# Two spectrum products in one instruction, with a new order of side jobs and ring slots, in an S4 and bilinear GLU block

## The chip, the cores and the metric

The kernel runs on one core of one Trainium2 chip. The metric is device time in microseconds for one execution. The kernel before takes 987.09 us, the median of three runs (984.9, 987.09 and 990.64).

## The reference

All inputs are fp32; there is one sequence of L = 2048 tokens with D = 640 channels, N = 192 complex states per channel and a hidden width F = 1536. Cut to what matters:

```python
mod = silu(c) @ w_mod                        # 640 -> 6 x 640: sa, ca, ga, sb, cb, gb
h = layernorm(x) * (1 + ca) + sa
# S4: for each channel d a kernel of 2048 taps, then a long convolution
P = exp(dt[d] * A[d, n] * l)                 # l = 0 .. 2047, complex
K[d, l] = Re(sum_n C[d, n] * P[d, n, l] * dt * B[d, n])
y = irfft(rfft(pad(h)) * rfft(pad(K)))[:2048] + h * Dskip
x = x + ga * y
h = layernorm(x) * (1 + cb) + sb
x = x + gb * (((h @ w_gate) * (h @ w_up)) @ w_down)
```

## The kernel before

The channels are worked in 5 blocks of 128 (db = 0 to 4). The program has four stretches.

**Start.** Constants, dt, seeds of the exponentials for channel block 0, loads of slices of w_mod, loads of rows of x. For a modulation vector, `mod_l` (L354) loads one third-dimension slice of w_mod, 1600 KB, into the memory that later holds a table (`t_tw` or `t_ti`), and `modrow` (L361) multiplies it on TensorE in two pieces, half 0 with 384 columns and half 1 with 256; ScalarE then copies each piece out.

**Kernel generation.** It has 40 steps, each for 16 channels; a step is three turns of the loop `for t in range(3*NK+24)` near L1335. In a step GpSimd forms outer products: the phases `Ph` as int32 and the magnitudes `EQ` and `EP` as fp32 (`outer`, L714), for the next step. ScalarE takes sines of the phases (`trig`, all ScalarE work is recorded at L230) into `tr`. VectorE multiplies sines by magnitudes into `QtA`, `PtA`, `QtB`, `PtB` (L769 to L796); L769 reads one operand twice through a broadcast. TensorE contracts over the states (L811 and L826). `Ph`, `EQ` and `EP` have two buffers each, so GpSimd waits where ScalarE or VectorE has not read them out. At the beginning of each channel block the seeds are made (`u_seeds`, 14 pieces on VectorE, ScalarE and TensorE, the last with three loads of ScalarE's activation table), and GpSimd doubles small tables from them (`tab_ph`, `tab_eq`).

**Side jobs.** All else of the convolution runs between these, as generators: each `yield` ends a piece. `u_stats` and `u_hm` load a block of 128 rows of x (320 KB), take its statistics on VectorE (L477) and store the normalised rows. `u_pre` (L853) is the first stage of the forward transform of the input, `u_g` (L899) its second, `u_k` (L838) the first stage of a kernel's transform. `u_c` (L919) does the second stage of the kernel's transform on TensorE (`stage2`, L893, which reads the table `t_tw`), the complex product with the input's spectrum on VectorE (L934 to L940), the first inverse stage on TensorE (L950), a copy on ScalarE and a store to `WD` in DRAM (L955). There are 16 whole ones and, for block 4, four that go in two halves. `u_d` (L958) reloads from `WD` (L963), does the last inverse stage (L971) and adds the residual (L978, or L975 into `xb`). `tables` (L1250) loads `t_tw`, once the last modulation slice there has been used.

The order is written out by hand in numbers. `SCHED` has a due time for each piece of each job; 60 units are a step, 20 a turn, and negative ones lie in the start. At each turn the pieces whose time has come are issued, in order of their numbers:

```python
(kg_aq, kg_ap, kg_b)[g](n)      # ScalarE: sines
due(2 * t)                      # side jobs
for f in MUL.pop(0): f()        # VectorE: products
due(2 * t + 1)                  # side jobs
kg_pool(n + 1, g)               # GpSimd: outer products, then TensorE
```

Each engine, and each engine's DMA queue, works in the order of issue. `SLOT` gives, letter by letter, which buffer of a ring the next tile of that name gets (`psf` in PSUM, `TV`, `gh`, `hf`, `W`, `xs`, `Kt` in SBUF); a tile waits until the last user of its buffer is done.

**Tail and GLU.** After the 40 steps 24 more turns (due times 2400 to 2880) do the rest of the convolution. Beside it the first weights are loaded by SP (`raw`, L1004, 640 KB), split into a high and a low part on ScalarE and VectorE (`split_g`, L1026), and the statistics of the first tokens taken (L1139). `split_g` of weight 1 also issues the next raw load. Then the GLU follows with its own hand-written order: products in L1078, L1502 and L1554 on TensorE.

In the product of a spectrum block, `kr` and `ki` are two PSUM tiles of 128 x 4 x dn (dn is 128, or 64 in block 4), `H` the input's spectrum and `T` a tile of the ring `TV`:

```python
V.tensor_tensor(T[:, 0], kr, H[:, 0], op=OP.mult)   # L934
V.tensor_tensor(T[:, 1], kr, H[:, 1], op=OP.mult)   # L935
V.tensor_tensor(kr, ki, H[:, 1], op=OP.mult)        # L936
V.tensor_tensor(ki, ki, H[:, 0], op=OP.mult)        # L937
V.tensor_tensor(x[:, 0], T[:, 0], kr, op=OP.subtract)
V.tensor_tensor(x[:, 1], T[:, 1], ki, op=OP.add)
```

## Time and profile before

| | us |
|---|---|
| median of the three runs | 987.09 |
| the profiled execution: its time | 988.54 |
| the profiled execution: its span | 986.8 |
| TensorE (PE) busy | 889.2 (90%) |
| VectorE (DVE) busy | 723.8 (73%) |
| ScalarE (ACT) busy | 579.4 (59%) |
| GpSimd (POOL) busy | 509.1 (52%) |

The span runs from the first to the last instruction on record; the time is the device's. The granted TensorE clock was 0.961 of full speed on the mean. The page cuts the span in 40 slices of 24.7 us and gives each engine's busy share as a digit in tenths. PEld is TensorE's weight load, which overlaps PE. In a row of a timeline stand the start, the duration, the engine, the line, the operation, the output and inputs with their shape, a count, and in brackets the idle time of the engine before it and what ended it. A name such as SPq or ACTq is a DMA issued by that engine.

### The profile page before, as it was taken

What the parts mean: (1) busy time and instruction counts of PE and PEld (TensorE: products, weight loads), DVE (VectorE), ACT (ScalarE), POOL (GpSimd) and SP (SyncE); (2) the same over time, 40 slices, a digit from 0 to 9 for tenths busy, and PEclk for the clock granted to TensorE, in tenths of its full rate; (3) what the DMA queues carried; (4) which work ended last, traced back from release to release, by engine and by line L of the source; (5) the groups of instructions that cost most, each with busy time, mean ns of one, the idle gap of its engine ahead of it and who ended that gap; (6) DMA issues with size and microseconds to landing.
All of it is one profiled execution on the core that took longest, in us unless ns stands there. A gap on an engine that the chain in (4) does not pass through costs nothing.

```text
span 986.8 us, 26765 instructions
## 1 busy us (share of the span) xinstructions
PE 889.2 (90%) x11134; PEld 720.2 (73%) x11134; DVE 723.8 (73%) x1400; ACT 579.4 (59%) x1076; POOL 509.1 (52%) x400
## 2 busy tenths in 40 slices
PE   4867898799789789988879999999999999999998
PEld 3565556586476557667736888889999788888998
DVE  8789568888978888794857665457676756578952
ACT  4869989987888887863336333334355443435430
POOL 5978899699879979960030354440113122222110
PEclk9877979999989889999999999999999999999999
DMA  7746654556246534658595665733564676658875
GB/s 254 262 142 223 204 194 147 172 165 185 77 153 181 152 105 126 205 172 257 189 273 191 222 191 182 242 125 113 184 217 124 197 231 222 222 179 292 237 244 187
DMA packets 158817, 188.54 MB, mean 191 GB/s; under 512 B 9828, under 2 KB 128360, under 8 KB 157544
## 3 DMA queue, kind: packets, MB, share of 16 engines
q1 hardware_dynamic: 149480, 155.51, 49.4%
q0 software_dynamic: 4752, 21.63, 7.6%
q10 hardware_dynamic: 4464, 9.70, 2.6%
q8 instruction: 87, 1.43, 0.6%
q14 instruction: 34, 0.28, 0.1%
HBM read 124.22 MB, written 62.59 MB: 189 GB/s over the span
## 4 chain that ended last, share of the span: by engine, by line
PE 55%; DVE 14%; ACT 12%; issue 10%; POOL 4%; DMA 3%; SPq 0%; DVEq 0%; POOLq 0%; ACTq 0%
PE pa L1078 18%; PE psg L1078 9%; PE pa L1502 9%; PE psfc L893 2%; PE kg L826 2%; PE kg L811 2%; PE psfa L893 2%; PE psfb L893 2%; ACT trb L230 1%; ACT tra L230 1%; PE psfc L950 1%; POOL EQ L714 1%; PE psfb L950 1%; PE pa L1554 1%; ACT L230 1%
## 5 line engine op out<-in xcount | busy, mean ns | idle before, releaser
L1055 POOL TENSOR_TENSOR tf<-wur,wgb 128x256 f32<-128x256 f32 x23 | 17.8, 775 | 246.9 <-DVE wtl L1026 199.5
L714 POOL TENSOR_TENSOR EQ<-LQ,RH 128x1536 f32<-128x1536 f32 x40 | 124.1, 3104 | 9.7 <-DVE QtB L771 9.5
L1026 DVE TENSOR_TENSOR wtl<-tf,wth 128x256 fp32r<-128x256 f32 (+1 forms) x72 | 36.7, 513 | 59.7 <-ACT wth L230 59.7
L714 POOL TENSOR_TENSOR Phb<-LH,DH 128x1536 int32<-128x1536 int32 x20 | 62.2, 3112 | 13.9 <-ACT tra L230 13.9
L714 POOL TENSOR_TENSOR EP<-LP,RH 128x768 f32<-128x768 f32 x40 | 66.0, 1650 | 0.0
L714 POOL TENSOR_TENSOR Pha<-LH,DH 128x1536 int32<-128x1536 int32 (+1 forms) x21 | 62.4, 2971 | 2.3 <-ACT trb L230 2.0
L1502 PE MATMUL pa<-wsg,sh 128*128 128x384 f32 (+1 forms) x304 | 58.4, 311 | 0.0
L826 PE MATMUL kg<-QtB,PtB 64*32 64x64 f32 x2560 | 48.7, 229 | 5.8 <-DVE QtB L770 5.3
L826 PEld LDWEIGHTS kg<-QtB,PtB 64*32 64x32 f32 x2560 | 41.7, 114 | 16.1 <-issue 7.2
L1502 PEld LDWEIGHTS pa<-wsg,sh 128*128 128x128 f32 x304 | 45.7, 189 | 0.0
L1541 POOL DMA_DIRECT2D wsg<-wdc x21 | 11.2, 531 | 66.5 <-PE pa L1554 35.6
L1026 DVE TENSOR_TENSOR wsg<-wga,wsg 128x640 fp32r<-128x640 f32 x36 | 33.7, 943 | 13.8 <-ACT wsg L230 13.8
L230 ACT ACTIVATE sh<-a 128x512 fp32r<-128x512 f32 x55 | 33.3, 625 | 13.9 <-PE psg L1554 6.2
L230 ACT ACTIVATE wsg<-wga 128x640 fp32r<-128x640 f32 x36 | 26.1, 730 | 25.0 <-PE pa L1502 12.8
L1026 DVE TENSOR_TENSOR sl<-a,sh 128x512 fp32r<-128x512 f32 x55 | 37.5, 702 | 4.0 <-ACT sh L230 4.0
L1078 PE MATMUL pa<-hh,wsg 128*128 128x512 f32 x150 | 40.2, 394 | 0.0
L1148 POOL TENSOR_SCALAR hfa<-xb,hr,hr 128x128 f32<-128x128 f32 x4 | 2.3, 577 | 67.5 <-DVE hr L283 67.5
L230 ACT ACTIVATE s<-pa 128x512 f32<-128x512 f32 x12 | 7.2, 598 | 48.5 <-PE pa L1078 48.5
L769 DVE TENSOR_TENSOR QtA<-tra,EQ 128x1024 f32<-128x1024 f32 x20 | 24.4, 1220 | 15.0 <-PE kg L811 7.0
L230 ACT ACTIVATE wth<-tf 128x256 fp32r<-128x256 f32 (+1 forms) x72 | 32.5, 481 | 4.9 <-DVE tf L1056 1.8
L230 ACT ACTIVATE a<-pa 128x512 f32<-128x512 f32 x12 | 7.2, 598 | 47.7 <-PE pa L1078 47.7
L1502 PE MATMUL pa<-wsg,sl 128*128 128x384 f32 (+1 forms) x152 | 34.4, 308 | 0.0
(656 smaller groups left out, 3125.6 us busy)
## 6 DMA issues: line engine op xcount, KB each, us to landing
wsg<-wdc POOLq DMA_DIRECT2D x21, 640.0 KB, 5.3
wgb<-B_w_gate SPq DMA_DIRECT2D x24, 320.0 KB, 4.6
wur<-B_w_up SPq DMA_DIRECT2D x24, 320.0 KB, 5.8
wsd<-wsg SPq DMA_DIRECT2D x12, 640.0 KB, 3.9
wga<-wdg SPq DMA_DIRECT2D x12, 640.0 KB, 3.9
wsg<-wsd POOLq DMA_DIRECT2D x12, 640.0 KB, 4.9
wdc<-xb SPq DMA_DIRECT2D x21, 320.0 KB, 3.3
TVb<-WD SPq DMA_DIRECT2D x22, 256.0 KB, 3.5
```

The lines of the kernel that those rows point to most:

```text
L230: return S.activation(o, i, f, **kw)
L714: G.tensor_tensor(o.rearrange("p x (h l) -> p x h l", l=8), lo.unsqueeze(2).to_broadcast([P, rows, nh, 8]), hi.rearrange("p h x -> p x h") ...
L769: return [lambda: V.tensor_tensor(Qt[:, :, :, 0:32], tr[:, :, :, ::-1], e[:, :, 0:32].unsqueeze(1).to_broadcast([P, 2, R, 32]), op=OP.mult ...
L811: PE.matmul(kg[j * 32 : j * 32 + 32, dd, :], PtA[:, c, dl * 4 + j, :], QtA[:, c, dl * 4 + j, :], start=dd == 0 and c == 0, stop=False, til ...
L826: PE.matmul(kg[j * 32 : j * 32 + 32, dd, :], PtB[lo : lo + 64, c, r, :], QtB[lo : lo + 64, c, r, :], start=False, stop=dd == 7 and c == 1, ...
L893: PE.matmul(r[c][par * 64 : par * 64 + 64, i, :], t_tw[:, k0 + k, c, :], src[:, k, :], start=True, stop=True, tile_position=(0, par * 64))
L950: PE.matmul(r[par][:, i], t_ti[lo : lo + 64, qd * 4 + i, c, :], x[lo : lo + 64, c, i, :], start=c == 0, stop=c == 1, tile_position=(lo, 0))
L1026: V.tensor_tensor(lo, v, hi, op=OP.subtract)
L1055: E.tensor_tensor(t[:, 0:2], u[:, 0:2], g[:, 0:2], op=OP.subtract)
L1078: PE.matmul(ps, w[a][:, k], x[b][:, l], start=first and n == 0 and m == 0, stop=n == 2 and m == len(ks) - 1, skip_group_check=True)
L1502: PE.matmul(AC[tb][t][c], x[:, ts], w[:, cs], start=st, stop=f == NF - 1 and n == 2 and (c == 0 or t % 2 == 1))
L1541: G.dma_start(WD[q], wdc[:, q // 3, q % 3])
```

## The change

In `u_c` the two products with `kr` become one instruction of double length, with `kr` read twice through a broadcast: 16 times 128 x 1024 in place of two of 128 x 512, and 8 times 128 x 512 in place of two of 128 x 256. In `SCHED` nearly every due time is new, and in `SLOT` most letters. The jobs themselves, their pieces and the order of pieces within a job stay as they were, and so does the GLU. What moves: in the start, half 0 of a modulation row (`mr`, third pair) comes before half 1, and the loads of two slices of w_mod (`ml`) come ahead of all blocks of x (`st`) but one; `t_tw` (`tab`) is loaded at 666 and not at 487, with the first `u_g` using it at 720 (before 710); of the three `u_c` products in steps 28 to 31 (block 2) one goes from 1688 to 1678 and one from 1919 to 1929, and the last seed pieces of block 4 (`q`, fourth row) from 1773, 1775 and 1800 to 1761, 1767 and 1818; kernel transform 37 goes ahead of step 40; in the tail the reloads of block 4 (`d`, last row) come at 2740 and 2765, before the second piece of weight work (`w`, fourth number, 2806).

```diff
@@ -29,148 +29,153 @@
 TURN = float(np.float32(2.0 * math.pi / 2.0**32 * (1.0 - 1.5e-7)))
 
 SCHED = dict(
-    ml=(-885, -929, -989),
-    mr=(((98, 154), (90, 130)), ((-884, 78), (-877, 73)), ((-885, -881), (-889, 132))),
+    ml=(-883, -955, -988),
+    mr=(((122, 153), (76, 101)), ((-878, 59), (-875, 116)), ((-888, -862), (-888, 22))),
     st=(
-        (-955, 11),
-        (-929, 195),
-        (-874, 149),
-        (-925, 128),
-        (-938, 121),
-        (-879, 152),
-        (-869, 167),
-        (-924, 162),
-        (-995, -925),
-        (-938, -871),
-        (-885, 93),
-        (-990, -871),
-        (50, 180),
-        (51, 214),
-        (-930, -878),
-        (-927, 39),
+        (-903, 20),
+        (-952, 164),
+        (-922, 78),
+        (-883, 75),
+        (-937, 55),
+        (-875, 104),
+        (-877, 153),
+        (-865, 126),
+        (-1003, -887),
+        (-944, -872),
+        (-934, 41),
+        (-950, -872),
+        (73, 158),
+        (153, 182),
+        (-947, -873),
+        (-911, 32),
     ),
...
-    rstd=(228, 229),
-    tab=(487, 829),
-    fo=(157, 189, 197, 222),
-    e0=(138,),
-    ds=(250, 255, 397, 411),
-    mc=((-872, 289, 307, 356, 356), (217, 378, 439, 446, 461), (309, 570, 620)),
+    rstd=(194, 195),
+    tab=(666, 794),
+    fo=(166, 179, 181, 182),
+    e0=(143,),
+    ds=(339, 319, 492, 204),
+    mc=((-866, 181, 279, 300, 324), (295, 337, 454, 508, 555), (343, 543, 593)),
     q=(
-        (-869, 185, 203, 222, 239, 309, 337, 355, 356, 357, 357, 358, 368, 369),
-        (338, 577, 594, 672, 676, 688, 718, 745, 812, 816, 825, 855, 872, 872),
-        (989, 1089, 1237, 1248, 1250, 1264, 1295, 1295, 1327, 1332, 1349, 1349, 1350, 1366),
-        (1298, 1403, 1490, 1732, 1735, 1735, 1746, 1763, 1773, 1775, 1778, 1800, 1830, 1835),
+        (-863, 160, 179, 224, 268, 273, 311, 316, 349, 349, 352, 352, 362, 369),
+        (448, 516, 635, 710, 717, 717, 722, 748, 800, 819, 822, 822, 833, 864),
+        (980, 1121, 1236, 1259, 1265, 1265, 1287, 1304, 1333, 1336, 1341, 1345, 1345, 1348),
+        (1286, 1415, 1599, 1728, 1737, 1737, 1746, 1751, 1761, 1767, 1786, 1818, 1828, 1837),
     ),
...
     c=(
-        ((814, 827, 901, 920), (780, 811, 971, 994), (1037, 1061, 1087, 1119), (912, 937, 1081, 1096)),
-        ((1383, 1400, 1462, 1484), (1183, 1207, 1352, 1373), (1331, 1337, 1371, 1385), (1104, 1141, 1221, 1239)),
-        ((1871, 1899, 2040, 2059), (1582, 1599, 1636, 1660), (1667, 1688, 1807, 1838), (1911, 1919, 2064, 2075)),
-        ((2088, 2090, 2133, 2146), (2187, 2210, 2277, 2289), (2348, 2351, 2395, 2412), (2295, 2310, 2343, 2346)),
-        ((2424, 2671, 2681, 2693, 2697, 2801), (2410, 2550, 2551, 2632, 2671, 2758), (2442, 2496, 2691, 2701, 2758, 2801), (2399, 2519, 2543, 2613, 2613, 2722)),
+        ((808, 828, 946, 946), (790, 815, 972, 994), (1053, 1064, 1091, 1108), (949, 963, 1081, 1087)),
+        ((1428, 1435, 1480, 1491), (1182, 1206, 1381, 1400), (1318, 1334, 1412, 1428), (1131, 1142, 1205, 1234)),
+        ((1863, 1885, 1973, 1991), (1603, 1603, 1622, 1668), (1643, 1678, 1816, 1830), (1915, 1929, 1997, 2036)),
+        ((2075, 2081, 2105, 2110), (2193, 2210, 2252, 2284), (2347, 2367, 2398, 2425), (2291, 2316, 2340, 2354)),
+        (
+            (2430, 2644, 2657, 2683, 2691, 2713),
+            (2401, 2563, 2601, 2602, 2642, 2666),
+            (2482, 2551, 2677, 2686, 2700, 2721),
+            (2373, 2457, 2610, 2636, 2664, 2667),
+        ),
     ),
     d=(
-        ((1839, 1887, 1907), (1356, 1450, 1450), (2879, 2879, 2879), (1143, 1182, 1199)),
-        ((1485, 1572, 1572), (1546, 1590, 1611), (1713, 1840, 1858), (1678, 1747, 1774)),
-        ((2151, 2257, 2269), (2245, 2320, 2328), (2323, 2396, 2422), (2119, 2149, 2168)),
-        ((2450, 2483, 2549), (2497, 2543, 2606), (2753, 2798, 2852), (2574, 2665, 2678)),
-        ((2816, 2835, 2861), (2847, 2876, 2876), (2862, 2877, 2878), (2876, 2879, 2879)),
+        ((1635, 1677, 1727), (1368, 1473, 1499), (2818, 2837, 2856), (1137, 1171, 1173)),
+        ((1760, 1801, 1806), (1548, 1610, 1645), (1827, 1897, 1958), (1712, 1729, 1763)),
+        ((2105, 2181, 2181), (2044, 2088, 2104), (2235, 2252, 2267), (2092, 2123, 2147)),
+        ((2523, 2558, 2589), (2586, 2612, 2634), (2720, 2767, 2813), (2609, 2709, 2724)),
+        ((2740, 2805, 2816), (2765, 2824, 2828), (2857, 2873, 2877), (2836, 2869, 2875)),
     ),
     k=(
...
-        (2504, 2534),
-        (2413, 2437),
-        (2492, 2495),
-        (2495, 2507),
...
+        (2446, 2513),
+        (2347, 2417),
+        (2519, 2586),
+        (2509, 2549),
     ),
...
-    w=(2508, 2575, 2790, 2776, 2819, 2829),
-    wl=(2444, 2450),
-    wm=(2801, 2834),
-    h=(2480, 2716, 2875, 2876, 2878, 2878, 2878, 2878),
...
+    w=(2456, 2588, 2714, 2806, 2783, 2709),
+    wl=(2554, 2672),
+    wm=(2795, 2810),
+    h=(2658, 2781, 2825, 2833, 2833, 2847, 2859, 2866),
...
-    Kt="abababaababbbabaabab",
...
-    W="abbababababababababababab",
...
+    W="ababababababababababababa",
...
-    xs="ababababababababbbab",
...
+    Kt="abababababbaabababab",
...
+    xs="ababababababababbaba",
 )
 SEG0 = ("l", "a", "b", "c", "ud", "r", "x", "e", "f", "G", "g", "D", "h", "v", "R", "")
 SEG = ("l", "a", "b", "c", "ud", "D", "r", "R", "x", "eE", "f", "g", "h", "v")
@@ -931,8 +936,7 @@
             need(1, "GH", db, qd)
             H = GH[db, qd][..., d0 : d0 + dn]
             T = ring(fp, [P, 2, 4, dn], "TV")
-            V.tensor_tensor(T[:, 0], kr, H[:, 0], op=OP.mult)
-            V.tensor_tensor(T[:, 1], kr, H[:, 1], op=OP.mult)
+            V.tensor_tensor(T, kr.unsqueeze(1).to_broadcast([P, 2, 4, dn]), H, op=OP.mult)
             V.tensor_tensor(kr, ki, H[:, 1], op=OP.mult)
             V.tensor_tensor(ki, ki, H[:, 0], op=OP.mult)
             x = T if parts == 1 else H
```

More of the change, by code (lines that the diff above doesn't have):

```diff
@@ new lines @@
+    hm=(
+        (46, 289),
+        (250, 415),
+        (276, 306),
+        (-1010, 384),
+        (-1007, 214),
+        (109, 286),
+        (92, 233),
+        (-871, 241),
+        (302, 355),
+        (228, 297),
+        (265, 316),
+        (201, 219),
+        (355, 512),
+        (241, 452),
+        (491, 539),
+        (373, 467),
+    ),
+    rstd=(194, 195),
[4 more added lines that the diff above has]
+    mc=((-866, 181, 279, 300, 324), (295, 337, 454, 508, 555), (343, 543, 593)),
```

106 lines of the change are left out of this document (45 added, 61 removed), and 20 rows, old and new, of tables (g, pre).

## The prediction

> **What bounds the kernel now.** I read the page's head and slices, then busy time by stage, then each engine's timeline and the chain of waits. The page:
>
> ```profile
> span 986.8 us, 26765 instructions
> ...
> POOL 5978899699879979960030354440113122222110
> ```
>
> GpSimd (POOL) is near full for 17 of 40 slices, about 24.7 us each, and light after that. The stages, with PE, PEld, DVE, ACT and POOL busy, then clock, DMA share and GB/s:
>
> ```profile
> 0.00:24.00 24.00, 9.87 (x37) 7.14 (x38) 19.52 (x86) 12.00 (x24) 12.19 (x26) 1.00 0.79 250
> 24.00:436.00 412.00, 348.66 (x7636) 256.91 (x7636) 346.60 (x619) 344.47 (x630) 371.99 (x222) 0.91 0.53 167
> 436.00:527.00 91.00, 75.38 (x1072) 54.55 (x1070) 58.42 (x154) 35.21 (x63) 9.36 (x15) 0.98 0.77 236
> 527.00:987.00 460.00, 455.33 (x2396) 401.55 (x2394) 299.22 (x544) 187.68 (x360) 115.58 (x138) 1.00 0.62 200
> ```
>
> The last 460 us, the GLU, are TensorE work (455 busy). The change touches none of it, so it counts at zero and moves only with its start. Three stages are left: the start, the 40 kernel-generation steps (24 to 436), and the tail between them and the GLU. In the generation GpSimd is busy 372 of 412 us (90%), the other three about 84% each. No GpSimd instruction is added or removed, so only its 40 idle us can be won there. The largest idle times (in brackets, with the releaser):
>
> ```profile
> 75.38 3.11 POOL L714 TENSOR_TENSOR EQ<-LQ,RH 128x1536 f32<-128x1536 f32 x1 [6.04 <-DVE QtB L771]
> 181.39 3.11 POOL L714 TENSOR_TENSOR Phb<-LH,DH 128x1536 int32<-128x1536 int32 x1 [5.95 <-ACT tra L230]
> 277.61 0.38 POOL L654 TENSOR_TENSOR DL<-ptb 128x96 int32<-128x96 int32 x1 [7.26 <-issue]
> 351.93 3.12 POOL L714 TENSOR_TENSOR Phb<-LH,DH 128x1536 int32<-128x1536 int32 x1 [6.35 <-ACT tra L230]
> ```
>
> Four waits make 25.6 of the 40 us. The last of them follows a block of seed work on ScalarE:
>
> ```profile
> 341.01 1.28 ACT L230 ACT_TABLE_LOAD   x1
> ...
> 349.89 1.28 ACT L230 ACT_TABLE_LOAD   x1
> 351.19 0.60 ACT L230 ACTIVATE tra<-Phb 128x512 f32<-128x512 int32 x1
> ```
>
> From 341.0 to 351.2 ScalarE makes seeds of the next channel block; the sines on which GpSimd's buffer hangs come behind them.
>
> **The change part by part.**
>
> **The merged product.** VectorE around the end of the generation:
>
> ```profile
> 437.36 1.22 DVE L769 TENSOR_TENSOR QtA<-tra,EQ 128x1024 f32<-128x1024 f32 x1
> 438.49 0.68 DVE L770 TENSOR_TENSOR QtA<-tra,EQ 128x512 f32<-128x512 f32 x1
> 439.09 0.68 DVE L771 SCALAR_TENSOR_TENSOR QtA<-tra,EQ 128x512 f32<-128x512 f32 x1
> 439.69 0.68 DVE L934 TENSOR_TENSOR TVa<-psfa,ghc 128x512 f32<-128x512 f32 x1
> 440.29 0.68 DVE L935 TENSOR_TENSOR TVa<-psfa,ghc 128x512 f32<-128x512 f32 x1
> 441.07 0.70 DVE L936 TENSOR_TENSOR psfa<-psfb,ghc 128x512 f32<-128x512 f32 x1
> ...
> 445.80 0.41 DVE L770 TENSOR_TENSOR QtB<-tra,EQ 128x256 f32<-128x256 f32 x1
> 446.13 0.41 DVE L771 SCALAR_TENSOR_TENSOR QtB<-tra,EQ 128x256 f32<-128x256 f32 x1
> ```
>
> Rows overlap by 0.08, so what an instruction occupies is the distance of starts: 1.13 us for 1024 elements (437.36 to 438.49), 0.60 for 512 (438.49 to 439.09), 0.33 for 256. Two of 512 take 1.20, one of 1024 takes 1.13: 0.07 saved, and the same for 2 x 0.33 against 0.60. With 16 full products and 8 half ones that is 24 x 0.07 = 1.7 us of VectorE. The first operand lies in PSUM and is read twice through a broadcast; L769 broadcasts as well, but from SBUF. L934, with its operand in PSUM, lasts as long as L770 without one, so I take the L769 price. From the other side, by full row durations, 2 x 0.68 - 1.22 = 0.14, or 3.4 us. If the broadcast from PSUM ran at half speed, it would be 24 x about 1 = +24 us of VectorE; nothing speaks for that. VectorE is busy 84% of the stage, so not all of it counts: I take -1.2 (0 to -3.4).
>
> [...]
>
> **The start.** Before the first sines ScalarE copies a modulation row, and in order behind it everything waits (timelines of TensorE, ScalarE and VectorE):
>
> ```profile
> 18.89 4.35 PE L361 MATMUL psfb<-t_tw,sil 128*128 128x256 f32 x10
> ...
> 26.50 0.48 ACT L230 ACTIVATE TVa<-psfa 1x384 f32<-1x384 f32 x1 [8.80 <-PE psfa L361]
> ...
> 30.14 1.23 DVE L769 TENSOR_TENSOR QtA<-trb,EQ 128x1024 f32<-128x1024 f32 x1 [3.70 <-ACT trb L230]
> ```
>
> The row copied is half 0; TensorE made half 1 before it (4.35 us). After the change half 0 comes first, so ScalarE is free up to 4.4 us sooner, and VectorE up to 3.7. Against it, both 1600 KB loads of w_mod now stand in SP's queue ahead of all x blocks but one, and ScalarE and VectorE get other side work in the first steps: by due times and durations ScalarE's load through step 5 goes from 63.2 to 64.9 us, VectorE's of steps 0 to 3 from 46.6 to 44.5. GpSimd's first long wait (6.04 at 75.38) would hand on what is won or lost. I take 0 (-2 to +3).
>
> **Steps 12 to 13 and the twiddle table.** The table t_tw for the spectra is loaded later: due 487 becomes 666, while its first use moves only from 710 to 720. The load before:
>
> ```profile
> 119.37 0.42 SPq L1250 DMA_DIRECT2D t_tw<-t_tw  x1
> ...
> DMA to landing us min/median/max: 9.0/9.0/9.0
> ```
>
> A step is 60 units and takes 412/40 = 10.3 us. The lead was 223 units (38 us) and becomes 54 (9.3 us): level with the 9.0 of the load, with x blocks and spectra beside it in SP's queue. If it is late, TensorE waits with the forward transforms queued behind; generation matmuls follow in the same queue. ScalarE's load in step 13 also grows, from 15.0 to 17.9 us, around the wait seen at 181.39. I take +1.5 for both (0 to +9.0).
>
> **The seed blocks.** Before the wait of 6.35 at 351.93 VectorE is full, and ScalarE too in its last part:
>
> ```profile
> 330.00:340.00 10.00, 9.51 (x261) 6.18 (x260) 9.62 (x19) 7.26 (x15) 10.00 (x5) 1.00 0.14 39
> 340.00:352.00 12.00, 3.18 (x28) 2.82 (x30) 11.86 (x22) 11.86 (x28) 5.65 (x4) 0.65 0.52 152
> ```
>
> By a count per step this place gets lighter: of the three spectrum products in steps 28 to 31 two move out, 7.2 us of VectorE (six instructions of 0.60 each). But a due time matters only by what it passes in a queue. The product before the wait goes from 1688 to 1678 and passes no set of step products on VectorE; the other goes from 1919 to 1929, behind the wait. The seed pieces on ScalarE (1773, 1775 and 1800 become 1761, 1767 and 1818) stay between the same sines. So I give this wait nothing (-3 to +3), and those at 75.38 and 277.61 nothing either, whose seeds also keep their turns. In the other steps loads move both ways: the sum over 40 steps of each step's largest engine load goes from 468.1 to 467.2 us by the same counting. New ring letters come with it; each can make or lift a wait of some us, and the trace of before can't show which.
>
> **The tail.** TensorE work, VectorE's queue and one reload meet. The rows are, in order, from the chain of waits, VectorE's timeline, a table by single us, SP's timeline, and the chain again:
>
> ```profile
> 449.94 0.88 PE psfb L848 x16
> ...
> 483.81 6.28 DVE L1139 BATCH_NORM_STATS2 a<-xb 128x6 f32<-128x128 f32 x32
> ...
> 490.00:491.00 1.00, 1.00 (x6) 0.84 (x5) 1.00 (x3) 0.25 (x1) 0.00 (x0) 1.00 0.00 0
> 491.00:492.00 1.00, 1.00 (x6) 0.81 (x6) 1.00 (x2) 0.00 (x0) 0.00 (x0) 1.00 0.00 0
> ...
> 491.57 0.37 SPq L1004 DMA_DIRECT2D wga<-B_w_gate  x1
> 492.11 0.95 SPq L963 DMA_DIRECT2D TVa<-WD  x2
> ...
> 492.57 5.63 DMA TVa<-WD
> ...
> 499.34 0.70 DVE xb L975
> ```
>
> SP issues the raw 640 KB of a weight, which waits for a buffer that VectorE frees behind the statistics at 483.81; the reload of the last block's spectrum (TVa<-WD) stands behind it in the same queue while the DMA engines are idle for two us, and takes 5.63 beside those 640 KB. The chain runs through it. After the change the first two reloads of block 4 (due 2740 and 2765) come ahead of the weight split that issues the raw load (2806), so they can start about 490.3, when the last store has landed, instead of 492.5. What is late next is VectorE itself: statistics, three splits and two adds in new order are over at about 483.9 + 13, while before the add that took the reload came at 499.34, that is 483.9 + 15.5. So -2.2 (0 to -4): the start of the reload and VectorE's queue both say this much. One kernel transform (L848, 0.88, with its gap 1.1) moves ahead of the generation's end: -1.1 (0 to -1.1). Two weight splits now stand on ScalarE ahead of the last copies to WD: up to +1.4, inside the range.
>
> [...]
>
> **Sum.** -1.2 + 0 + 1.5 + 0 - 2.2 - 1.1 = -3.0. The profiled execution took 988.54 (1.7 above its span), so 985.5; it stood 1.45 above the median of 987.09, so on the median **984.1 us**.
>
> **The rivals.**
>
> *The waits in the generation close.* For it: four waits hold 25.6 us, no step's largest load grew much, and a full VectorE or a ring slot hands its delay on to GpSimd, so a changed neighbour of a seed block can shorten them. Against it: the seed blocks that cause them keep their turns. Between a quarter and a half of 25.6 is 6.4 to 12.8, the middle 9.6: 974.5.
>
> *Nothing gained.* GpSimd is the bound of the generation at 90%, so VectorE's merge is hidden; and in the tail VectorE may be late whatever the reload does. Left are -1.1 and +1.5: 987.5. A merge that saves nothing because the broadcast from PSUM costs its 0.07 belongs here: 985.3 with the rest as forecast.
>
> *Slower: the x blocks come late.* Two 1600 KB loads stand ahead of them, with 9.0 us to landing for one (the row above). The list of DMA issues for the other and for x blocks, then SP's and VectorE's timelines:
>
> ```profile
> t_ti<-w_mod SPq DMA_DIRECT2D x2, 1600.0 KB, 8.7
> f16a<-A_u SPq DMA_DIRECT2D x4, 320.0 KB, 8.5
> ...
> 9.22 0.43 SPq L354 DMA_DIRECT2D t_tw<-w_mod  x1
> ...
> 23.82 0.89 DVE L477 BATCH_NORM_STATS2 st<-ghb 128x6 f32<-128x320 f32 x2
> ```
>
> Statistics of four blocks stand on VectorE, in order, ahead of the last seeds and the first products. One after the other, 9.2 + 9.0 + 8.7 + 8.5 = 35.4 is the landing, against 23.82: 11.6 late, and with VectorE as releaser of the 6.04 wait it goes through: 995.7. It decides at 23.8: each us beyond is one of time. Against it: the first 24 us moved 250 GB/s on the mean, and two loads and five blocks (4.9 MB) need only 19.6 us at that, from 8: 27.6, or +3.8 and 987.9.
>
> **How the numbers follow.** 0.5% (4.9 us) is about what a measurement of this kernel can tell from no change: faster is below 982.2, slower above 992.0. The forecast has 0.36 (own range 980 to 988; 0.09 of it faster, 0.27 within). The closing of waits has 0.27, all faster. Nothing gained has 0.13, all within. Late transfers, with new ring letters that cost some us counted there, have 0.24, of which 0.22 lies above 992.0 and 0.02 within. So faster 0.36, same 0.42, slower 0.22. The range runs from 972 to 994: about 0.08 of the second case and 0.11 of the last are left out.
>
> **What would show it.** Right: L934 x24 with 1.2 us at 1024 elements and no L935; reloads of block 4 ahead of the raw weight, no idle DMA there; GpSimd's four waits within 3 us of what they were; the GLU at 460 us, starting near 524. Wrong: first products later than 30.1 us; TensorE waiting for t_tw; new GpSimd waits over 3 us; L934 over 1.3 us.

## The result and the profile after

The kernel after takes 993.52 us in the median (10 runs, 990.22 to 997.65) and the kernel before, beside it, 987.11 us (10 runs, 984.26 to 990.66). The ratio is 1.0062, with an interval of 1.0039 to 1.0084: slower by 0.6%, where the forecast was faster by 0.3%. A second series of the same two kernels gave 991.30 against 987.81, 1.0040 (1.0025 to 1.0056). The time lies inside the stated range and on its wrong side. That the range holds it is luck: its part above 992 stands for late transfers and new ring letters, and not for what is found below.

The profiled execution of the kernel after, 996.98 us, is one of its longer ones, so a second profile of it, of an execution of 990.73 us, is read beside it. In the new code the products of a spectrum block are at L939 to L945, and the lines named in the prediction lie 4 or 5 lower down.

The page's head and slices, then two groups of instructions (the last columns are busy time and mean ns, then the idle time before them and what ended it):

```profile
span 995.2 us, 26725 instructions
...
POOL 5978999799779959980021254440113122222110
...
L719 POOL TENSOR_TENSOR EQ<-LQ,RH 128x1536 f32<-128x1536 f32 x40 | 124.1, 3103 | 8.7 <-DVE QtB L776 8.5
...
L719 POOL TENSOR_TENSOR Phb<-LH,DH 128x1536 int32<-128x1536 int32 x20 | 62.3, 3114 | 22.2 <-ACT tra L235 22.2
```

Before, the same two groups had:

```profile
L714 POOL TENSOR_TENSOR EQ<-LQ,RH 128x1536 f32<-128x1536 f32 x40 | 124.1, 3104 | 9.7 <-DVE QtB L771 9.5
...
L714 POOL TENSOR_TENSOR Phb<-LH,DH 128x1536 int32<-128x1536 int32 x20 | 62.2, 3112 | 13.9 <-ACT tra L230 13.9
```

GpSimd does the same work in the same time, and waits 8.3 us longer ahead of the phases `Phb`, for a sine on ScalarE (1.0 us less ahead of `EQ`). The table by stage:

```profile
0.00:24.00 24.00, 9.82 (x33) 6.09 (x34) 17.64 (x81) 12.00 (x24) 12.24 (x26) 1.00 0.79 263
24.00:436.00 412.00, 344.69 (x7404) 253.02 (x7402) 339.64 (x599) 337.98 (x618) 364.61 (x220) 0.90 0.54 166
436.00:527.00 91.00, 78.19 (x1276) 60.02 (x1272) 64.15 (x152) 38.82 (x70) 17.41 (x18) 0.94 0.70 215
527.00:987.00 460.00, 456.11 (x2399) 400.29 (x2396) 301.80 (x545) 191.13 (x365) 115.49 (x138) 1.00 0.63 204
```

The generation stage holds 364.61 us of GpSimd's work where it held 371.99: 7.4 us of it have not been done by 436, and the other three engines have 4.0 to 7.0 us less there as well. The GLU is as it was: from its first ScalarE copy of a product to the end of the span it takes 463.7 us, before 463.3. So the loss is made ahead of it, and most of it in the generation. GpSimd's longest waits in it, from its timeline, can be set against the four that the prediction shows:

```profile
73.25 3.11 POOL L719 TENSOR_TENSOR Phb<-LH,DH 128x1536 int32<-128x1536 int32 x1 [7.18 <-ACT tra L235]
86.96 3.11 POOL L719 TENSOR_TENSOR EQ<-LQ,RH 128x1536 f32<-128x1536 f32 x1 [2.67 <-DVE QtB L776]
...
181.10 3.11 POOL L719 TENSOR_TENSOR Phb<-LH,DH 128x1536 int32<-128x1536 int32 x1 [4.78 <-ACT tra L235]
...
262.08 3.12 POOL L719 TENSOR_TENSOR Phb<-LH,DH 128x1536 int32<-128x1536 int32 x1 [2.41 <-ACT tra L235]
...
279.73 0.36 POOL L713 COPY LQ<-RL 128x96 f32<-128x96 f32 x1 [7.53 <-DVE RL L653]
...
355.89 3.11 POOL L719 TENSOR_TENSOR Phb<-LH,DH 128x1536 int32<-128x1536 int32 x1 [7.47 <-ACT tra L235]
...
366.62 0.36 POOL L713 COPY LQ<-RL 128x96 f32<-128x96 f32 x1 [2.96 <-DVE RL L653]
```

The seeds of blocks 1 and 2 (73 to 181) end nearly level, 0.5 more together. The seeds of block 3 (260 to 280) cost more, and those of block 4 (from 345) most of all: the wait at 355.89 has grown by 1.1, and 10.7 us behind it stands a wait of 2.96 that was not there. The table of the experiments below sums these waits by seed block for each kernel: block 4 goes from 6.35 to 10.43, block 3 from 10.38 to 12.24, the rest from 19.96 to 21.00. These are sums of one execution each, and they vary: up to 255 us, where 15 of the profiles below have the same order and the same product, the waits from 30 us on sum to between 18.9 and 22.6 us.

GpSimd's last outer product ends 7.7 us later than before in the first profile and 6.2 in the second. From there the second profile wins back 3.8 us up to the GLU (its first ScalarE copy of a product is 2.4 us late), the first nothing (8.0 late). The 6.2 is as was expected of the second profile (5.5 to 7); at the GLU about 5 was expected, and 2.4 was found.

### The profile page after: what moved, and what is told of

Its sections match the earlier page's. It is cut to its first block, busy times and chain, and to the rows that moved or that the text cites. A ratio compares the mean times of both kernels' runs of the same rounds, so it can differ in the third digit from the quotient of the medians.

```text
span 995.2 us, 26725 instructions
## 1 busy us (share of the span) xinstructions
PE 893.6 (90%) x11134; PEld 724.0 (73%) x11134; DVE 724.3 (73%) x1376; ACT 579.9 (58%) x1076; POOL 509.7 (51%) x400
## 4 chain that ended last, share of the span: by engine, by line
PE 58%; ACT 11%; issue 9%; DVE 9%; DMA 5%; POOL 1%; SPq 0%; DVEq 0%; POOLq 0%; ACTq 0%
PE pa L1082 18%; PE psg L1082 9%; PE pa L1506 8%; PE kg L831 2%; PE psfa L898 2%; PE kg L816 2%; PE psfc L898 1%; PE psfb L898 1%; PE psfc L877 1%; ACT trb L235 1%; PE psfa L877 1%; PE psfa L954 1%; ACT L235 1%; ACT tra L235 1%; PE psfc L853 1%
## 5 line engine op out<-in xcount | busy, mean ns | idle before, releaser
L774 DVE TENSOR_TENSOR QtA<-tra,EQ 128x1024 f32<-128x1024 f32 x20 | 24.4, 1220 | 18.9 <-ACT tra L235 4.6
L1152 POOL TENSOR_SCALAR hfc<-xb,hr,hr 128x128 f32<-128x128 f32 x4 | 2.2, 555 | 66.4 <-DVE hr L288 66.4
```

The costliest lines, as they stand in the source:

```text
L774: return [lambda: V.tensor_tensor(Qt[:, :, :, 0:32], tr[:, :, :, ::-1], e[:, :, 0:32].unsqueeze(1).to_broadcast([P, 2, R, 32]), op=OP.mult ...
```

## The experiments

The theory was that the order of jobs on TensorE and ScalarE at the seeds of blocks 3 and 4 holds GpSimd up. Its rivals: the merged product is slower than two (by its operand in PSUM, read through a broadcast); GpSimd's own order, two tables made ahead of each other, is at fault; the steps of that stretch simply hold more TensorE work; the loss is the tail's. The new ring letters are a further rival, and no run tests them apart from the due times. Where an expectation calls a theory by a letter, the words beside it hold.

All results in one table. The ratio is against the kernel before in the same series; the last three columns are worked out from one profile each, as the sum of the bracketed waits in GpSimd's timeline at 255 to 290 (seeds of block 3), 340 to 380 (block 4) and behind 380.

| kernel | median, us | ratio (interval) | block 3 | block 4 | later |
|---|---|---|---|---|---|
| before | 987.11 | 1 | 10.38 | 6.35 | 0 |
| after | 993.52 | 1.0062 (1.0039 to 1.0084) | 12.24 | 10.43 | 0.58 |
| after, second series | 991.30 | 1.0040 (1.0025 to 1.0056) | 11.64 | 10.73 | 0 |
| merge_only | 984.40 | 0.9977 (0.9959 to 0.9995) | 9.96 | 4.51 | 0 |
| order_only | 993.97 | 1.0069 (1.0047 to 1.0091) | 10.93 | 9.25 | 0 |
| seed_first | 993.04 | 1.0064 (1.0044 to 1.0084) | 11.15 | 12.07 | 0 |
| tables_swapped | 993.38 | 1.0054 (1.0033 to 1.0076) | 11.11 | 9.10 | 0 |
| transform_later | 994.21 | 1.0082 (1.0049 to 1.0116) | 11.23 | 6.41 | 4.22 |
| inject | 988.50 | 1.0010 (0.9987 to 1.0033) | 10.68 | 5.78 | 0 |
| copy_later | 994.55 | 1.0074 (1.0051 to 1.0096) | 13.83 | 8.80 | 0 |
| copy_last | 991.58 | 1.0051 (1.0028 to 1.0074) | 10.41 | 8.72 | 0 |
| step30_light | 998.62 | 1.0112 (1.0085 to 1.0140) | 10.38 | 7.78 | 8.44 |
| both | 999.29 | 1.0127 (1.0093 to 1.0160) | 12.80 | 7.45 | 7.77 |
| stretch_light | 996.68 | 1.0093 (1.0071 to 1.0115) | 10.44 | 9.88 | 3.19 |
| stretch_light_copy | 997.81 | 1.0098 (1.0076 to 1.0120) | 12.20 | 10.79 | 2.81 |
| copy28_later | 992.38 | 1.0049 (1.0027 to 1.0071) | 10.23 | 8.75 | 0.49 |
| copy28_transform | 996.25 | 1.0071 (1.0044 to 1.0099) | 11.62 | 8.70 | 4.53 |
| copies_transform | 998.16 | 1.0088 (1.0062 to 1.0114) | 10.78 | 7.20 | 4.59 |
| residual_early | 998.85 | 1.0119 (1.0090 to 1.0148) | 10.38 | 8.62 | 0.52 |
| reload_first | 986.02 | 0.9982 (0.9959 to 1.0005) | 10.50 | 4.37 | 0 |

### Which half of the change

`merge_only` is the kernel before with nothing but the merged product; `order_only` is the kernel after with two products in its place.

```diff
-            V.tensor_tensor(T[:, 0], kr, H[:, 0], op=OP.mult)
-            V.tensor_tensor(T[:, 1], kr, H[:, 1], op=OP.mult)
+            V.tensor_tensor(T, kr.unsqueeze(1).to_broadcast([P, 2, 4, dn]), H, op=OP.mult)
```

> The kernel before with its own due times and ring letters; only the two products with kr become one. Theory A (the time is lost by the new order, at places where ScalarE copies a TensorE result out ahead of seed pieces or sines): about 986, that is -1.2 against before (0 to -1.7), instructions of 1.19 to 1.23 us in place of pairs of 0.60, no new wait of GpSimd. Theory B (the merged product itself costs the time, through its broadcast read of PSUM): 993 or more, with GpSimd waiting behind VectorE.

> The kernel after with the two products as they were before: new due times and ring letters only. Theory A: 993 to 995, GpSimd's waits as after the change (7.5 at 356, 3.0 at 367, 2.4 at 262). Theory B: 987, as before.

The merge alone is faster by 0.23% (3.0 us between the medians), and the order alone is as slow as the whole change. So the merge is innocent, and all of the loss is the order's, due times and ring letters together. `merge_only` is the fastest kernel of the study: it beats before and after. In the new order the merge is worth nothing that can be measured (993.97 without it, 993.52 and 991.30 with it).

### The seeds of block 4

In the new order three jobs stand in TensorE's queue ahead of the small transposes of block 4's seeds (L535, due 1818), from which VectorE makes the tables that GpSimd doubles. TensorE's timeline after, first row and last of each job:

```profile
355.64 1.94 PE L816 MATMUL kg<-QtA,PtAb 128*32 128x64 f32 x64
...
357.94 1.06 PE L975 MATMUL psfb<-TVb,ct 64*32 64x512 f32 x8
358.93 0.64 PE L877 MATMUL psfc<-hfb,ct 64*64 64x512 f32 x1
...
360.97 0.49 PE L954 MATMUL psfb<-TVa,t_ti 64*128 64x128 f32 x2
...
363.40 0.38 PE L954 MATMUL psfc<-TVa,t_ti 64*128 64x128 f32 x2
363.71 0.49 PE L535 MATMUL psfa<-ct,prm 128*128 128x128 f32 x2
...
365.43 0.49 PE L535 MATMUL psfa<-ct,pta 128*128 128x128 f32 x2
```

and before:

```profile
352.70 1.65 PE L811 MATMUL kg<-QtA,PtAb 128*32 128x64 f32 x64
...
354.52 0.47 PE L530 MATMUL psfc<-ct,prm 128*128 128x128 f32 x2
...
358.20 0.49 PE L530 MATMUL psfc<-ct,pta 128*128 128x128 f32 x2
```

Before, the transposes start 2.6 us behind GpSimd's `Phb` (351.93); after, 7.8 us behind it (355.89), with a last inverse stage (L975, 1.0 us), an input transform (L877, 2.0) and a first inverse stage (L954, 2.7) ahead of them. VectorE, though, makes the tables only behind a second set of transposes, that of `pta`, and this one started 6.3 us behind `Phb` before and starts 9.5 us behind it after (365.43): the first inverse stage stood ahead of it before, too (L950, between the two sets). So 3.3 us of the 5.2 count here, about what the last inverse stage and the input transform take. GpSimd has three outer products to do meanwhile and is free at 366.62 - 2.96 = 363.66, before the second set starts.

Three edits of the kernel after try this place. `seed_first` puts ScalarE's copies of that input transform (block 3, part 2) behind the seeds; `tables_swapped` lets GpSimd make its phase table ahead of its magnitude table; `transform_later` puts the whole transform behind the seeds.

```diff
-  (1764, 1802, 1814)
+  (1764, 1802, 1819)     seed_first
+  (1764, 1838, 1839)     transform_later
...
-  low=((..., 1873, 2097), (..., 1862, 2112))
+  low=((..., 1862, 2097), (..., 1873, 2112))     tables_swapped
```

> The kernel after; one due time is changed, the last piece of the input transform of block 3, rows 2 (1814 to 1819), so that ScalarE takes the seed piece of block 4 (1818) before the two copies of that transform. Theory A: the seed piece no longer waits for TensorE, the small tables are ready earlier, GpSimd's wait of 2.96 before the copy of LQ goes to about 0, and the time falls by 3.0 to 990.5. Theory C (GpSimd loses those 3 us because it makes the magnitude table ahead of the phase table): the wait stays, 993.5.

> The kernel after with the two small tables of the first half of block 4 in the order of before on GpSimd: phase table (1862) ahead of magnitude table (1873). Theory C: the 2.96 us go, 990.5. Theory D: both tables hang on the last seed piece, 0.35 us apart, so only the name of the waiting instruction changes, and the time stays at 993.5.

> The kernel after; the last two pieces of the input transform of block 3, rows 2, go from 1802 and 1814 to 1838 and 1839, behind the last seed pieces of block 4, on TensorE as well as on ScalarE (near their places of before, 1834 and 1865). Theory D (what counts is the work ahead of the seeds' small transposes in TensorE's queue; the ScalarE order alone made no difference): the seeds come 2 to 3 us earlier, GpSimd's wait before the copy of LQ near 367 falls from 2.96 to under 1, and the time by 2 to 3 to about 991. Theory C (GpSimd's own order of the two small tables): the wait stays, 993.5.

The first two change nothing: in `seed_first` the new wait is still 2.42 us, in `tables_swapped` it only has another name, `DL<-ptb` with 2.49. The transform on TensorE is what counts for this wait: in `transform_later` it falls to 1.00 us. The other profiles bear that out: with the transform ahead of the transposes nine profiles of the new order have 2.08 to 2.96 us here, with it behind them seven have 0.45 to 1.00. The wait before it, for the sines, is 5.08 us here, but 6.34 to 8.43 in the other six of the seven, so that one is not the transform's. And the median does not follow. GpSimd's timeline in `transform_later`:

```profile
353.86 3.11 POOL L716 TENSOR_TENSOR Phb<-LH,DH 128x1536 int32<-128x1536 int32 x1 [5.08 <-ACT tra L232]
...
362.63 0.35 POOL L710 COPY LQ<-RL 128x96 f32<-128x96 f32 x1 [1.00 <-DVE RL L650]
...
390.29 3.11 POOL L716 TENSOR_TENSOR Pha<-LH,DH 128x1536 int32<-128x1536 int32 x1 [3.72 <-ACT trb L232]
```

and its ScalarE and VectorE:

```profile
365.22 0.60 ACT L232 ACTIVATE hfa<-psfc 128x512 f32<-128x512 f32 x1 [4.31 <-PE psfa L874]
```

```profile
368.47 0.69 DVE L798 TENSOR_TENSOR PtB<-trb,EP 128x512 f32<-128x512 f32 x1 [5.54 <-ACT trb L232]
```

The same VectorE product in the kernel after:

```profile
367.83 0.69 DVE L801 TENSOR_TENSOR PtB<-trb,EP 128x512 f32<-128x512 f32 x1 [0.92 <-ACT trb L235]
```

Now the copy (1839) stands in ScalarE's queue directly behind its TensorE piece (1838) and ahead of the next sines. ScalarE stands still for 4.31 us, VectorE behind it for 5.54, and at a later buffer GpSimd pays 3.72. Of 11.0 us of waits at and behind this seed block 10.6 are left. The two rows of VectorE show where the gain went: its copy to `RL` comes 4.0 us sooner than in the kernel after (362.24 against 366.23), but the product behind it no sooner. From there both kernels run level, and GpSimd starts its `Pha` at 390.29 and 390.47. In the kernel before, the copy of this transform is due at 1865, 31 units behind its TensorE piece at 1834. This combination was not tried in the new order.

`inject` is the test from the other side: `merge_only` with that one transform moved ahead of the seeds.

```diff
-  (..., 1834, 1865)
+  (..., 1799, 1806)     inject
```

> The kernel before with the merged product (984.4), and one thing taken over from the new order: the input transform of block 3, rows 2, goes from 1834 and 1865 to 1799 and 1806, on TensorE ahead of the seeds' transposes of block 4 (1800) and of the product behind them. Theory D: the seeds come 2 to 2.5 us later, GpSimd waits for them near 360 where it did not, and the time is 2 to 2.5 higher, 986.5. If TensorE's queue has slack there, 984.4.

GpSimd's timeline in `merge_only`, then in `inject`:

```profile
349.76 3.12 POOL L714 TENSOR_TENSOR Phb<-LH,DH 128x1536 int32<-128x1536 int32 x1 [4.51 <-ACT tra L230]
...
357.97 0.39 POOL L654 TENSOR_TENSOR DL<-ptb 128x96 int32<-128x96 int32 x1
```

```profile
347.22 3.11 POOL L711 TENSOR_TENSOR Phb<-LH,DH 128x1536 int32<-128x1536 int32 x1 [3.71 <-ACT tra L227]
...
357.41 0.39 POOL L651 TENSOR_TENSOR DL<-ptb 128x96 int32<-128x96 int32 x1 [2.07 <-issue]
```

The transform alone makes a wait of 2.07 us where the three other profiles of the old order have none. That a TensorE job ahead of the seeds' transposes makes GpSimd wait about 2 us for its tables is so shown from both sides. That the generation gets longer by it is not: the waits at this seed block sum to 5.78 us, within the 4.37 to 6.35 of those three, and GpSimd's last outer product ends at 431.61, in `merge_only` at 432.22. The median is 988.50 against 984.40, in another series each; by the ratios that is 0.33% more, and the intervals just overlap. The profiled executions, 985.48 and 984.80 us, do not show where it is spent.

### The seeds of block 3

Both pieces of kernel transform 19 are due at 1294 in the new order, ahead of the sines that the wait at 262.08 is for. ScalarE after:

```profile
260.13 0.60 ACT L235 ACTIVATE f16b<-psfc 128x512 f32<-128x512 f32 x1 [3.93 <-PE psfc L853]
...
261.34 0.60 ACT L235 ACTIVATE tra<-Phb 128x512 f32<-128x512 int32 x1
```

ScalarE waits 3.93 us for a transform that TensorE has only just been given, and the sines stand behind the copy. Of the 3.93 the transform's own matmuls are 1.1; before them TensorE finishes generation products:

```profile
257.26 1.80 PE L831 MATMUL kg<-QtB,PtB 64*32 64x64 f32 x64
258.99 1.09 PE L853 MATMUL psfc<-ct,Ktb 128*64 128x128 f32 x16
```

`copy_later` and `copy_last` move it to two places behind.

```diff
-        (1294, 1294),
+        (1338, 1339),     copy_later
+        (1352, 1353),     copy_last
```

> The kernel after; kernel transform 19, whose TensorE piece and ScalarE copy are both due at 1294, goes to 1338 and 1339, behind the exponentials of the seeds of block 3 (its PSUM letter stays). Theory A: ScalarE's stall of 3.9 before the copy at 260 goes, GpSimd's wait at 262 falls from 2.4 to about 0.8, and the time by 1.6 to 991.9. If the wait at 262 has another cause (the sines behind a full VectorE), it stays and the time is 993.5.

> The kernel after; kernel transform 19 goes from 1294 (both pieces) to 1352 and 1353, behind the seeds' transposes of block 3 as well as behind the sines. At 1338 it took 0.9 from GpSimd's wait at 262 and put 2.4 on the one at 280. Theories D and E: wait at 262 about 1.5 (2.4), wait at 280 as before the move or less (7.5), time -1 to 992.5. If the 2.4 at 280 came from elsewhere, it is there again: 994.5.

At 1338 it stands ahead of the transposes of block 3's seeds: the wait at 262 is 1.55, and that for the seeds 9.98, where it is 6.6 to 7.7 in all other profiles. This is the same mechanism as in block 4. At 1352 it stands behind them: 1.50 and 6.61, and 10.41 for block 3. But that can't be put down to the move. The four kernels with 1352 have 10.41, 10.78, 12.20 and 12.80 for block 3, and the eleven profiles of the kernel after and of its variants that leave this transform at 1294 have 10.23 to 12.24, with a middle value of 11.11; the four of the old order have 9.96 to 10.68. So the growth at block 3 is some 0.7 us by the middle values, and not the 1.9 of the first profile. The time of `copy_last`, 991.58, lies 1.9 us under the first series of the kernel after and level with the second (991.30): no gain is shown.

### Less TensorE work, and moves together

`step30_light` takes two transforms out of the step with the seeds of block 4, `stretch_light` an input transform and a kernel transform out of the whole stretch; `both` and `stretch_light_copy` add `copy_last` to them. `copy28_later` moves only the copy of kernel transform 28, and the two others add `transform_later`, then `copy_last`.

```diff
-  (1764, 1802, 1814)   (1765, 1839, 1851)
+  (1764, 1838, 1839)   (1765, 1930, 1932)     step30_light, both
+  (1764, 1838, 1839)   (1950, 2040, 2042)     stretch_light, stretch_light_copy
...
-  (1883, 1894)   (2016, 2106, 2134)
+  (2056, 2058)   (2043, 2106, 2134)     stretch_light, stretch_light_copy
...
-  (1933, 1938)
+  (1933, 1955)     copy28_later, copy28_transform, copies_transform
...
-  (1764, 1802, 1814)
+  (1764, 1838, 1839)     copy28_transform, copies_transform
...
-  (1294, 1294)
+  (1352, 1353)     both, stretch_light_copy, copies_transform
```

> The kernel after, with TensorE relieved around step 30: the last two pieces of two input transforms leave it (block 3, rows 2: 1802 and 1814 to 1838 and 1839; block 4, rows 1: 1839 and 1851 to 1930 and 1932). Theory E (TensorE is the bound from step 30 to 34: 17.5 of 18.8 us busy after the change, 13.8 of 15.7 before; what was won by the move of one transform was lost again at ScalarE's wait for TensorE near 386): GpSimd's wait near 367 under 1, no new wait at 390, the generation ends 3 to 4 us earlier, 990. Theory D alone (only the queue ahead of the seeds' transposes counts): as in the run with one transform moved, 993 to 994.

> The kernel after with the moves of the two runs before it together (two transforms out of step 30, kernel transform 19 behind the seeds of block 3). Theories D and E: -4 to -5, 989, and about 2 above the kernel before with the merged product alone, for what is lost at the start of the generation. If the loss is spread over the whole order, at most -1: 992.5.

> The kernel after, with TensorE relieved over the whole stretch from step 30 to 33: the input transform of block 3, rows 2, at 1838 and 1839 as before in this study; that of block 4, rows 1, at 2040 and 2042 (1839 and 1851); kernel transform 29 at 2056 and 2058 (1883 and 1894; the kernel before had 2069 and 2083); one load of x rows for block 4 follows from 2016 to 2043. Theory E (TensorE is the second bound of the stretch, behind the seeds; moving work to step 32 made it worse, 8.1 us of waiting at 393): the wait for the seeds near 363 under 1 and no wait over 1 us near 390, the generation ends 3 to 5 us earlier than after the change, time 989 to 990.5. If the transforms were only moved to a place where they cost the same: 993.5 or more.

> The same, and kernel transform 19 at 1352 and 1353 (1294), the one move that gave time by itself (991.6). If the two places are independent: 1.5 to 2 below the run with the stretch alone, 987.5 to 989.

> The kernel after, unchanged, beside the two on the same chip, and a second profile of it: all theories 993.5; the first profile was of an execution of 996.98, so this one should show the generation's end 5.5 to 7 later than before and the GLU's start about 5 later.

> The kernel after; only ScalarE's copy of kernel transform 28 goes from 1938 to 1955, behind the next set of sines. In the kernel after it waits 4.8 us at 387 (a spectrum product on VectorE, then the transform on TensorE, in the PSUM buffer that the product frees), with the sines behind it. Theory F (ScalarE's in-order copies right behind their own TensorE piece hold the sines up): ScalarE's wait goes, but GpSimd does not wait there in the kernel after, so the time falls little: 993 (0 to -1) against 991.3 to 993.5.

> The same with the input transform of block 3, rows 2, behind the seeds (1838 and 1839), which alone shortened GpSimd's waits for the seeds by over 4 us and lost it again near 390. Theory F: GpSimd's wait near 363 stays at 1 or less and no wait over 1 us comes near 390; the generation ends 3 to 4 us earlier than after the change (+2.5 to +4 against before), time 988 to 990. If what is lost near 390 is TensorE's or VectorE's own work: 993 as with the transform alone.

> The same, and kernel transform 19 at 1352 and 1353 (1294). Theory F: 1 less than the run before it, 987 to 989; if not independent, no less.

The six with the transform at 1838 and 1839 are slower than the kernel after, by 2.7 to 5.8 us in the median. Each has the ScalarE stall of `transform_later` again, of 4.31 us to the hundredth. In `step30_light` and `both` the second transform, whose pieces I put at 1930 and 1932, makes a stall of its own in the same way (6.91 us and 5.84 us), and GpSimd pays 8.11 us at 393 and 7.31 at 394. Less TensorE work in the stretch brought nothing, but these kernels all carry the stall, so they say little on the amount by itself. Moves that had shortened a wait singly did not add up. `copy28_later` is level with the kernel after, where the copy waits 4.83 us ahead of the sines. In the two kernels that add the transform to it GpSimd still pays 4.21 and 4.27 us near 391: they have the 4.31 us stall as well, and the copy, though behind one set of sines, still waits (3.42 and 3.49 us) ahead of the set `trb` that GpSimd waits for. So there the expectation that ScalarE's wait would go failed, and what would follow from it was not tested. What `after_again` showed is told above.

### The tail

`residual_early` moves the last-inverse job of block 0, part 2, out of the tail (2818 to 2254), with one new letter of the ring `xs`, 12 of `TV` and 44 of `psf`; it is the kernel after otherwise. `reload_first` is `merge_only` with the raw load of a weight moved behind the reloads of block 4.

```diff
-  (2818, 2837, 2856)
+  (2254, 2275, 2280)     residual_early
...
-  w=(2508, 2575, 2790, 2776, 2819, 2829)
+  w=(2508, 2575, 2790, 2848, 2819, 2829)     reload_first
```

> The kernel after; the last inverse stage of block 0, rows 2, which stands among those of block 4 at the end (2818 to 2856), goes into the generation (2254 to 2280), and the ring of two residual buffers gets letters in which no load of the last block waits for a store. Theory: the GLU starts late because the load for the last add waits for a store of 5.1 us into which its buffer goes (521.9 to 527.0); without it the last add comes 2 to 3 us earlier behind the end of the generation (about +5.5 instead of +8.0 against before), and the time is 990.5 to 991.5. If VectorE or the weights set the GLU's start, it stays at 993.5.

> The kernel before with the merged product (984.4), and one due time changed: the split of weight 1, which also issues the raw load of 640 KB, goes from 2776 to 2848, behind the first two reloads of block 4. This is the tail step of the prediction alone. As predicted: -2.2 (0 to -4), so 982.2. Rival: the reload waits for the last store of its spectrum to land (4.4 us after its issue in the kernel after), so only 0.5 us is to be had, 984 or, with the split now late for the GLU, more.

`residual_early` ends slower, 998.85, though GpSimd ends its generation 5 us sooner than in the kernel after: around its end, at 434 to 440, TensorE now waits 3.19 us for a reload, VectorE 5.12 and ScalarE 5.88 behind it. With that, and with its new letters, it says nothing on the tail. `reload_first` is the clean one. SP's queue in it, then in `merge_only`:

```profile
485.93 1.87 SPq L962 DMA_DIRECT2D TVa<-WD  x2
...
493.31 0.51 SPq L1003 DMA_DIRECT2D wga<-B_w_gate  x1
...
495.05 2.22 SPq L962 DMA_DIRECT2D TVa<-WD  x2
```

```profile
488.90 0.37 SPq L1003 DMA_DIRECT2D wga<-B_w_gate  x1
489.44 0.95 SPq L962 DMA_DIRECT2D TVa<-WD  x2
```

Counted from VectorE's last spectrum product, the reload starts 2.2 us sooner and its add comes 2.4 us sooner: the -2.2 of the forecast. But from that product to the GLU it is 39.0 us in the one and 38.9 in the other. The chain of waits in `reload_first` points to the reason: the raw load now stands ahead of the next reload, and the chain runs through that one.

```profile
493.31 0.51 SPq L1003
...
495.05 5.51 DMA TVa<-WD
```

## Why the prediction was wrong, step by step

**The seed blocks: here it failed.** The prediction gave these waits nothing (-3 to +3), as the seed pieces "stay between the same sines" or "keep their turns". In the kernel after GpSimd's generation ends 6.2 to 7.7 us late, and of the 7.0 us that its waits grew in the first profile 4.1 are at block 4's seeds and 1.9 at block 3's. I wrote that a due time matters only by what it passes in a queue, and then asked this of VectorE's products and ScalarE's seed pieces only. TensorE's queue I did not ask: two products of 1678 and 1929 were followed, an input transform from 1834 to 1802, ahead of transposes due at 1818, was not, nor a last inverse stage from 1572 to 1801. Of the growth at block 4 about 2 us are so explained, the new wait for the tables. The count of loads per step was blind to it, since a step's load doesn't tell what stands ahead of what; `inject` makes the wait with one job moved within a step. The signs named in the prediction were blind to it as well: all four waits stayed within 3 us of what they were, and the new one, 2.96, is just under the 3 that were to show a fault. I also said that ring letters could make such waits and not be seen; the wait for the tables is one of queue order, and could have been seen in the due times. What of the growth at 355.89 itself (1.1 to 1.9 us) is due to which job was not shown: ScalarE reaches its first table load of this seed block 4.3 us behind the start of GpSimd's `Pha` where it was 3.2, and no run isolates why. So the order as a whole is shown to cost all of the 6 to 8 us; for about 2 of them a place and a reason are shown, and how the rest comes about is open. No move that was tried removes the loss; which set of moves would is open.

**The merged product: right.** The row of the form is as forecast:

```profile
L939 DVE TENSOR_TENSOR TVa<-psfa,ghb 128x1024 f32<-128x1024 f32 x3 | 3.7, 1224 | 0.8 <-PE psfa L898 0.8
```

1.22 us at 1024 elements, as in the rows of L774 whose operands lie in SBUF (1.22 on the mean): in these durations the broadcast from PSUM costs nothing. By `merge_only` it is worth 0.05 to 0.41%, 0.5 to 4.0 us, against -1.2 (0 to -3.4). Starts in a full VectorE queue are 1.32 us apart from the merged product to the next and 1.38 for the two before (326.69 to 328.01 and 328.80 to 330.18): 0.06 x 24 = 1.4 us of VectorE's own time, and by durations 3.4. The interval holds both.

**The start: right (0).** The row copy comes 1.9 us sooner and the first product 1.75 sooner:

```profile
24.60 0.48 ACT L235 ACTIVATE TVa<-psfb 1x384 f32<-1x384 f32 x1 [6.85 <-PE psfb L366]
```

```profile
25.86 0.89 DVE L482 BATCH_NORM_STATS2 st<-ghb 128x6 f32<-128x320 f32 x2
...
28.39 1.22 DVE L774 TENSOR_TENSOR QtA<-trb,EQ 128x1024 f32<-128x1024 f32 x1
```

The rival's late x blocks are there, 2.0 us (23.82 to 25.86), on VectorE directly ahead of that product, and past its point of decision: but they only took back part of the 3.7 us that the earlier row copy won.

**The twiddle table: +1.5 not needed.** It was issued at 143.47 and first used, with no wait, 11.9 us later:

```profile
143.47 0.56 SPq L1254 DMA_DIRECT2D t_tw<-t_tw  x1
```

```profile
155.40 0.44 PE L898 MATMUL psfa<-ghc,t_tw 128*64 128x128 f32 x4
```

The lead came out 2.6 us longer than the 9.3 that I read from 54 units. Near 181 GpSimd's wait fell, from 5.95 to 4.78.

**The tail: -2.2 - 1.1 = -3.3 forecast, -3.8 in the second profile, +0.3 in the first.** Sign and size can come out as forecast; the cause is borne out only in part. The reload stands ahead of the raw load, as said:

```profile
499.10 0.91 SPq L967 DMA_DIRECT2D TVa<-WD  x2
...
507.15 0.92 SPq L1008 DMA_DIRECT2D wga<-B_w_gate  x1
```

But its first load still waits for the last store to `WD`, and starts 8.16 us behind VectorE's last product where it was 8.63: 0.5 us of the 2.2. That store was issued 3.7 us behind the product in both kernels, and the reload started 4.4 us after the issue, in `reload_first` 2.8 us; why it took longer is not shown. `reload_first` has the 2.2 in full and gains nothing by it. What was late next was not VectorE, as I wrote, but the end of the same queue; in the kernel after it is this row of the chain of waits, a load of x2 that follows a store of it:

```profile
521.90 5.12 DMA x2d<-xsa
...
527.03 2.88 DMA xsa<-A_u
```

Where the second profile's 3.8 us come from is therefore not shown, beyond the transform moved ahead (1.1). The granted TensorE clock from the end of the generation to the GLU was 0.98 before, and 0.94 and 0.96 in the two profiles after; what that is worth is not shown either.

**The sum** was -3.0. The two profiles have +7.7 and +6.2 at the end of the generation, merge, start and table included, and +0.3 and -3.8 from there: +8.0 and +2.4 at the GLU, beside +6.4 and +3.5 in the medians of the two series. Of the rivals none had this mechanism; "late transfers, with new ring letters" had the sign, and the closing of waits had the place, a changed neighbour of a seed block, with the sign the wrong way round.

## What to carry to other kernels

When an order of jobs is changed, take each engine's queue in turn and list what newly stands ahead of the short steps that a nearly full engine waits for; loads summed per step don't show it. A copy out of PSUM placed right behind its own matmuls, ahead of work that others wait for, holds its engine until TensorE has worked off its queue up to the end of these matmuls (3.93 and 4.31 us here, of which the matmuls themselves were 1.1 and 3.0): leave work between the two, and enough of it, as behind one set of sines a copy that had waited 4.83 still waited 3.42 and 3.49 in two kernels. And change the instruction apart from the order: here the smaller half alone was faster, and the larger half hid it.

## What was not expected of the hardware

One kernel's executions spread more than the effects under study: before gave 982.45 to 992.80 us in one series of 23, 1% from end to end, and the two profiles of the kernel after differ by 6.2 us in span at a mean granted clock of 0.954 and 0.956. Of these, 4.1 us lie between the end of GpSimd's generation and the GLU. A profile of one execution is therefore good for the places of waits, and for a wait that comes again in every profile, but not for a sum to a few us.
